# Attention on TensorE in pairs of steps, in a fused linear-attention and mixture-of-experts kernel

## The chip, the cores and the metric

The kernel runs on one core of one Trainium2 chip. The metric is device time in microseconds: three runs of the kernel before gave 607.51, 609.04 and 610.86 us, a median of 609.04. One further execution was profiled.

## What is computed

Linear attention over 8 batches of 8 heads (576 rows of 64 values each), and then a mixture of experts with one expert per row on its output. The change touches the attention alone:

```python
def phi(x):
    proj = np.einsum('bhsd,df->bhsf', x, w_phi)                 # 64 -> 128 features
    proj = proj - np.max(np.abs(proj), axis=-1, keepdims=True)
    return np.concatenate([np.exp(proj), np.exp(-proj)], axis=-1)
q_p, k_p = (phi(q), phi(k))
kv = np.einsum('bhsf,bhsd->bhfd', k_p, v)                       # sums over the rows
z = np.sum(k_p, axis=2)
num = np.einsum('bhsf,bhfd->bhsd', q_p, kv)
den = np.einsum('bhsf,bhf->bhs', q_p, z)[..., None] + 1e-06
return (num / den).astype(np.float32)
```

The rows of this go to the expert stage: a skip score and a gate choose the rows and their expert, and two matrix products with a ReLU between them follow. All matrix products of the attention are in float32.

## The kernel before

**Units, items and steps.** A unit is four heads of one batch, of k or of q; there are 16 of each. Every unit has five items: item 0 is the tail of 64 rows, items 1 to 4 are the rest. The loop at L760 goes through steps t. In each step an item of the k stream and, six steps later in its own unit, an item of the q stream pass through six stages, each with a lag (`lag` in `CFG`). The letters of `order` ('EPAZUT') give the order inside a step:

- T (L748, `st_t`): VectorE transposes the loaded rows into `xT` (L322, L324), and the next unit's load is issued on SyncE's queue.
- P, one step later (`st_proj`, L327): TensorE projects the k item and the q item into one tile `ps_P` of two banks (L347; 32 matrix instructions in the trace, 24 where one of the two is a tail). VectorE takes the largest absolute value (`m`, L354) and subtracts it (`u`, L357). There are two such tiles.
- E, three steps after T: for k, ScalarE takes the exponentials (`ek`, L372 and L373) and GpSimd sums them into `z` (L380 to L386). For q, TensorE first transposes `u` into the one bank `ps_U` (L393), and ScalarE takes the exponentials from there (`eq`, L399 and L400).
- U, four steps after T: for k, the kv sums (L415, L422) into the one bank `ps_K`; ScalarE copies them out as `kvs` at the unit's end (L426). For q, the numerators and denominators (L513, and L492 for the tails of two batches together) into a bank `ps_O`; VectorE divides in four instructions (`den`, `rec`, `xm`, `lgm`, L464 to L476). There are two banks `ps_O`.
- Z, at item 4 of k, five steps after T (L433): sums of `z` over the partitions, into a bank `ps_O`, copied by ScalarE as `zs` (L436).
- A, at item 4 of k, six steps after T (`st_aug`, L438): for each of two halves, products of `kvs` with the gate's columns and a transpose of `zs` into a bank `ps_O` (L446, L450), which two instructions of ScalarE copy into `kva` (L451, L454). The numerators of the unit's q items need both halves.

Z falls on steps 9, 14, 19, and so on, A on steps 10, 15, 20, and so on. After the last item of a batch comes work on the gate (`post`, L541): small instructions of VectorE at once, and `rank` and `index` four and seven steps later, from the list `later`.

**What sets the order.** From step 8 to step 78 TensorE's instructions stand in the order in which the loop writes them (`manual_schedule` for that engine alone). The other engines' instructions are put in order by a scheduler that estimates times and takes what it holds to be ready first. Every engine then works through its own list in that order.

**Shapes on the array.** The trace names with each matrix instruction the part of the array it uses: the projections 64\*64, the kv sums and numerators 128\*64, the sums of Z 128\*32, and the transposes, A and the gate's products 128\*128.

Of the kernel before, what the change touches and what calls it, by code (L numbers as in the profile page):

```python
# [18 lines left out]
P = 128  # L19
SLOT = 256  # L20
CFG = {'late': 1, 'gp': (0, 1, 2, 4, 6, 8, 9, 11, 12, 14, 17, 19, 21), 'rows': 9.0, 'tab': (2, 4, 5, 6, 6, 7, 8, 9, 10, 11, 12, 13, 16, 20, 32), 'ql': -2, 'q1': 0, 'vtl': 3, 'at': 6, 'cp': 0, 'seq': ('E', 'E', 'E', 'C', 'C', 'SC', 'C', 'DS', 'C', 'D'), 'lag': (1, 3, 4, 5, 6), 'post': (4, 7, 7), 'man': (8, 79), 'dnow': 0, 'off': 6, 'order': 'EPAZUT', 'direct': (), 'nb': {'K': 1, 'P': 3, 'U': 2, 'O': 2}, 'na': {'K': 1, 'P': 2, 'U': 1, 'O': 2}, 'apools': (('ld', 2), ('hl', 5), ('up', 3), ('zp', 2), ('ep', 7), ('kvp', 6), ('ac', 1), ('xp', 2)), 'mpools': (('rawp', 1), ('mx', 2), ('wseta', 1), ('mo', 2), ('wsetb', 1), ('rawq', 1))}
# [3 lines left out]
def kernel(  # L25
# [13 lines left out]
    B, H, S, D = q.shape  # L39
    NF = w_phi.shape[1]  # L40
    E = w_gate.shape[1]
# [214 lines left out]
    with actx:  # L256
# [17 lines left out]
        for b in range(B):  # L274
            for kind in ("k", "q"):
                for hq in range(NQ):
                    u = Unit()
# [19 lines left out]
        def st_loadv(u):  # L297
            u.v = ld.tile([P, 4, 4 * D], F32, tag="v", name="v", bufs=3)
            u.vt = vts[u.g % 3]
            for h in range(4):  # L300
                nc.sync.dma_start(
                    out=u.v[:, h, :].rearrange("p (g c) -> p g c", c=D),
                    in_=vu[u.g, 0:4 * P, h, :].rearrange("(g p) c -> p g c", p=P))

        def st_loadvt(u):
            for pr in range(2):
                r = slice(pr * 64, pr * 64 + 64)
                nc.sync.dma_start(
                    out=u.vt[r, pr], in_=vu[u.g, 4 * P:S].rearrange("p (n r) c -> p r n c", r=2)[:, pr])
# [409 lines left out]
        later = []  # L719
        now = [0]  # L720
# [5 lines left out]
        LP, LE, LU, LZ, LA = CFG["lag"]  # L726
# [9 lines left out]
        def run_stage(lag, f):  # L736
            for items, us, off in streams:
                s = now[0] - off - lag
                if 0 <= s < n:
                    f(*items[s])  # L740
# [7 lines left out]
        def f_t():  # L748
            for items, us, off in streams:
# [3 lines left out]
                if 0 <= s < n:  # L753
                    u, i = items[s]
                    st_t(u, i)
                    if i == 0 and s // 5 + 1 < len(us):
                        st_load(us[s // 5 + 1])

        man = None
        for t in range(n + OFF + LA):  # L760
            if CFG["man"] and t == CFG["man"][0]:
                man = ExitStack()
                man.enter_context(tc.manual_schedule(engines={mybir.EngineType.PE}))
            if CFG["man"] and t == CFG["man"][1]:
                man.close()
            now[0] = t
            for w, f in [x for x in later if x[0] <= t]:
                later.remove((w, f))
                f()
            for c in CFG["order"]:  # L770
                if c == "Z":
                    run_stage(LZ, st_z)
                elif c == "A":
                    run_stage(LA, st_aug)
                elif c == "U":
                    run_stage(LU, f_use)
                elif c == "E":
                    run_stage(LE, f_exp)
                elif c == "P":
                    st_proj()  # L780
                else:
                    f_t()
            run_stage(LU - 3, lambda u, i: st_loadv(u) if (i == 0 and u.kind == "k") else None)
            run_stage(CFG["vtl"], lambda u, i: st_loadvt(u) if (i == 0 and u.kind == "k") else None)
            if t == CFG["at"]:
                setup_aug()
            if t == 1:
                setup()
# [505 lines left out]
```

## Time and profile before

| what | value |
|---|---|
| three runs, median | 607.51, 609.04, 610.86; 609.04 us |
| the profiled execution's own time | 607.91 us |
| its span (first to last instruction) | 605.7 us |
| granted TensorE clock, mean | 0.989 |
| attention on TensorE (last numerators) | to about 341 us of the span |
| steps 10 to 75, by the groups of A | 30.22 to 288.17 us |

Times within the execution count from the span's start. A matrix instruction's duration in the trace overlaps with the next one's, so what a group of them costs is read from its start to the start of the next group. TensorE runs every float32 product as two instructions, so a count in the trace is twice that of the program's order.

### The profile page before, as it was taken

The numbers are of one execution on the slowest core, as the hardware profiler recorded it, in microseconds if no ns is written. First come the engines' busy times: TensorE is split into PE (matmuls) and PEld (weight loads), VectorE is DVE, ScalarE is ACT, GpSimd is POOL, SyncE is SP. The second block draws the span as 40 slices with busy tenths as digits, with TensorE's granted clock in tenths as the row PEclk, the third lists the DMA queues.
The fourth block names the chain that finished last, engine by engine and source line by source line (L and its number), as shares of the span: only waits on it lengthen the run. The fifth ranks groups of instructions, "written<-read, shape, count | busy, mean of one in ns | idle before, by whom it ended". The sixth has DMA issues, their size and how long they took to land. (4 is left out here: it accounts for less than half of the span.)

```text
span 605.7 us, 18767 instructions
## 1 busy us (share of the span) xinstructions
PE 567.1 (94%) x7486; PEld 466.3 (77%) x7486; DVE 502.6 (83%) x1085; ACT 330.7 (55%) x649; POOL 375.9 (62%) x399
## 2 busy tenths in 40 slices
PE   4799999999999899998989799899999998999993
PEld 2477777777777677776766699798998987988892
DVE  5799998999999989999998749956788887867841
ACT  3366565555555565564643645344557765656720
POOL 5665585495666775847865644995576674738021
PEclk9999999999999999999999999899999999999997
DMA  9998898896677567621235297489677788868500
GB/s 159 156 164 149 182 194 179 163 211 121 149 160 155 138 135 170 158 74 46 73 120 185 69 302 277 167 278 321 201 260 240 242 288 297 269 198 261 194 19 30
DMA packets 250233, 108.33 MB, mean 179 GB/s; under 512 B 192417, under 2 KB 235553, under 8 KB 250144
## 3 DMA queue, kind: packets, MB, share of 16 engines
q1 hardware_dynamic: 245632, 97.58, 62.1%
q0 software_dynamic: 3200, 9.45, 4.3%
q8 instruction: 60, 0.98, 0.7%
q10 hardware_dynamic: 1312, 0.08, 0.1%
q14 instruction: 29, 0.24, 0.1%
HBM read 83.86 MB, written 24.02 MB: 178 GB/s over the span
## 5 line engine op out<-in xcount | busy, mean ns | idle before, releaser
L380 POOL TENSOR_TENSOR z<-ek 128x512 f32<-128x512 f32 x64 | 81.2, 1272 | 77.0 <-ACT ek L373 54.3
L200 POOL TENSOR_TENSOR w<-wraw_c,w 128x256 fp32r<-128x256 f32 x108 | 97.5, 935 | 47.5 <-ACT w L195 43.9
L195 ACT ACTIVATE w<-wraw_c 128x1024 fp32r<-128x1024 f32 x96 | 97.9, 1051 | 6.9 <-DMA wraw_c<-in_moe_w_dram 6.5
L200 DVE TENSOR_TENSOR w<-wraw_c,w 128x1024 fp32r<-128x1024 f32 x69 | 90.2, 1321 | 9.5 <-ACT w L195 7.6
L354 DVE TENSOR_REDUCE m<-ps_P 128x8 f32<-128x1024 f32 (+2 forms) x86 | 88.5, 1030 | 7.1 <-PE ps_P L347 7.1
L357 DVE TENSOR_TENSOR u<-ps_P,m 128x1024 f32<-128x1024 f32 (+2 forms) x86 | 88.8, 1032 | 2.9
L347 PE MATMUL ps_P<-wsrc,xT 64*64 64x128 f32 x2048 | 79.4, 282 | 11.4 <-DMA raw<-in_k_dram 7.2
L513 PEld LDWEIGHTS ps_O<-kva,eq 128*64 128x64 f32 x2048 | 74.0, 136 | 16.4 <-issue 5.8
L513 PE MATMUL ps_O<-kva,eq 128*64 128x74 f32 x2048 | 77.4, 228 | 3.9 <-DVE lgm L476 3.8
L347 PEld LDWEIGHTS ps_P<-wsrc,xT 64*64 64x64 f32 x2048 | 57.4, 135 | 28.1 <-issue 19.2
L399 ACT ACTIVATE eq<-ps_U 128x512 f32<-128x512 f32 x64 | 37.9, 592 | 64.8 <-PE ps_U L393 64.3
L415 PE MATMUL ps_K<-ek,v 128*64 128x256 f32 x512 | 71.2, 396 | 0.0
L879 POOL DMA_INDIRECT out_dram<-o,si x22 | 34.3, 1558 | 56.6 <-DVE si L878 50.1
L946 PE MATMUL ps_O<-w,hh 128*128 128x512 f32 x160 | 64.0, 400 | 0.0
L633 POOL TENSOR_SCALAR OP<-iota_p,rkp,wcol 128x128 bf16<-128x128 f32 x62 | 48.4, 790 | 24.0 <-DVE RKH L636 17.9
L372 ACT ACTIVATE ek<-u 128x512 f32<-128x512 f32 x64 | 40.4, 631 | 39.0 <-DVE u L357 23.0
L393 PE MATMUL ps_U<-ident,u 128*128 128x128 f32 x288 | 48.9, 287 | 2.7 <-DVE u L357 2.4
L324 DVE STREAM_TRANSPOSE xT<-raw 128x512 f32<-128x512 f32 x64 | 44.7, 702 | 6.1 <-DMA raw<-in_k_dram 3.3
L415 PEld LDWEIGHTS ps_K<-ek,v 128*64 128x64 f32 x512 | 32.0, 137 | 21.1 <-issue 10.8
L950 PE MATMUL ps_O<-w,hh 128*128 128x512 f32 x120 | 47.2, 394 | 0.1
L951 PE MATMUL ps_O<-w,hlo 128*128 128x512 f32 x120 | 47.0, 392 | 0.0
L384 POOL TENSOR_TENSOR z<-z 128x512 f32<-128x512 f32 x32 | 40.7, 1273 | 2.5
(254 smaller groups left out, 1202.0 us busy)
## 6 DMA issues: line engine op xcount, KB each, us to landing
wraw_c<-in_moe_w_dram SPq DMA_DIRECT2D x96, 512.0 KB, 5.4
raw<-in_k_dram SPq DMA_DIRECT2D x64, 144.0 KB, 3.1
raw<-in_q_dram SPq DMA_DIRECT2D x64, 144.0 KB, 4.5
v<-in_v_dram SPq DMA_DIRECT2D x64, 128.0 KB, 2.8
out_dram<-xm SPq DMA_DIRECT2D x16, 512.0 KB, 6.2
xrows<-xm SPq DMA_DIRECT2D x8, 516.0 KB, 3.8
xrows<-xm SPq DMA_DIRECT2D x8, 512.0 KB, 4.2
vt<-in_v_dram SPq DMA_DIRECT2D x32, 32.0 KB, 2.5
```

The costliest lines, as they stand in the source:

```text
L195: nc.scalar.activation(out=hi, in_=raw, func=AF.Copy)
L200: eng.tensor_tensor(out=lo[:, r], in0=raw[:, r], in1=hi[:, r].bitcast(F32), op=ALU.subtract)
L347: nc.tensor.matmul(p[s * 64:s * 64 + 64, hd, (nj + j) * NF:(nj + j + 1) * NF], xT[r, g * P + s * 64:g * P + s * 64 + 64], wsrc[r], start=T ...
L354: nc.vector.tensor_reduce(out=m.rearrange("p (j h) -> p j h", h=2), in_=pv, axis=AX.X, op=ALU.max, apply_absolute_value=True)
L357: nc.vector.tensor_tensor(out=uu[:, 0:2 * nj, :].rearrange("p (j h) f -> p j h f", h=2), in0=pv, in1=m.rearrange("p (j h o) -> p j h o", h ...
L380: zeng.tensor_tensor(out=z, in0=e[:, 0:2, :], in1=e[:, 2:4, :], op=ALU.add)
L393: nc.tensor.transpose(t[:, tt * P:(tt + 1) * P], uu[:, tt, :], ident)
L415: nc.tensor.matmul(o[hd * 64:hd * 64 + 64, :], u.v[:, 2 * hd + pr, g * D:(g + 1) * D], u.e[i][:, 2 * j + hd, :], start=(g == 0), stop=False,)
L513: nc.tensor.matmul(ov[s * 64:s * 64 + 64, 2 * j + hd, :], e[:, half, j, hd, s * 64:s * 64 + 64], kva[:, half, 2 * pr + hd, :], start=(half ...
L633: (nc.vector if last else nc.gpsimd).tensor_scalar(out=OP[:, t0 + t, c, :], in0=iota_p, scalar1=rkp[:, t:t + 1], scalar2=wcol[:, NT:NT + 1 ...
L946: nc.tensor.matmul(y[sub], hh[:, t], wh[:, fi, :], start=first, stop=False)
L950: nc.tensor.matmul(y[sub], hh[:, t], wl[:, fi, :], start=False, stop=False)
```

## The change

Steps 8 to 77 are written in pairs (t even, then t+1) instead of one by one. The list `PAIR` gives the order within a pair: a letter is a stage, and 0 or 1 is the step. L stands for the due functions of the list `later`, D for the loads of v; both were outside the list before.

```diff
+        PAIR = [('L', 0), ('T', 0), ('T', 1), ('E', 0), ('P', 0), ('P', 1), ('L', 1), ('E', 1), ('A', 0), ('Z', 0), ('Z', 1), ('U', 0), ('A', 1), ('U', 1), ('D', 0), ('D', 1)]
...
-            now[0] = t
-            for w, f in [x for x in later if x[0] <= t]:
-                later.remove((w, f))
-                f()
-            for c in CFG["order"]:
-                if c == "Z":
+            first = 8 <= t < 78 and (t - 8) % 2 == 0
+            if 8 <= t < 78 and not first:
+                continue
+            for c, dt in PAIR if first else [(c, 0) for c in "L" + CFG["order"] + "D"]:
+                now[0] = t + dt
+                if c == "L":
+                    for w, f in [x for x in later if x[0] <= now[0]]:
+                        later.remove((w, f))
+                        f()
+                elif c == "Z":
...
+                elif c == "D":
+                    run_stage(LU - 3, lambda u, i: st_loadv(u) if (i == 0 and u.kind == "k") else None)
+                    run_stage(CFG["vtl"], lambda u, i: st_loadvt(u) if (i == 0 and u.kind == "k") else None)
                 else:
                     f_t()
-            run_stage(LU - 3, lambda u, i: st_loadv(u) if (i == 0 and u.kind == "k") else None)
-            run_stage(CFG["vtl"], lambda u, i: st_loadvt(u) if (i == 0 and u.kind == "k") else None)
```

No instruction is added or taken away. The arithmetic and the buffers are the same; the names' numbers and the line numbers (six more from L759 on) differ.

**Place 1: ScalarE at the A of step 20, the first step of a pair.** Before: `u_1051` is the `u` of step 19, `kva_1143` what A makes in step 20 from its two halves `ps_O_1144` and `ps_O_1150`.

```order
L399 ACTIVATE eq_1119<-ps_U_1114 128x512
L400 ACTIVATE eq_1119<-ps_U_1114 128x512
L372 ACTIVATE ek_1195<-u_1051 128x4x128
L373 ACTIVATE ek_1195<-u_1051 128x4x128
L451 ACTIVATE kva_1143<-ps_O_1144 128x4x73
L454 ACTIVATE kva_1143<-ps_O_1144 128x4
L451 ACTIVATE kva_1143<-ps_O_1150 128x4x73
L454 ACTIVATE kva_1143<-ps_O_1150 128x4
```

With the change, `u_1157` is the `u` of step 20 itself, from the first projection of this very pair; the halves of A are `ps_O_1191` and `ps_O_1197`:

```order
L399 ACTIVATE eq_1187<-ps_U_1182 128x512
L400 ACTIVATE eq_1187<-ps_U_1182 128x512
L451 ACTIVATE kva_1190<-ps_O_1191 128x4x73
L454 ACTIVATE kva_1190<-ps_O_1191 128x4
L372 ACTIVATE ek_1275<-u_1157 128x4x128
L373 ACTIVATE ek_1275<-u_1157 128x4x128
L451 ACTIVATE kva_1190<-ps_O_1197 128x4x73
L454 ACTIVATE kva_1190<-ps_O_1197 128x4
```

The copies of A's second half now stand behind exponentials of the same pair's first projection; before, both halves stood behind exponentials of the step before. All seven A on even steps read like this.

VectorE's list from the end of the pair of steps 18 and 19 to that `u`, with the change (`ps_O_1037` and `ps_O_1060` are the numerators of those two steps, `ps_P_1138` the first projection of the pair of steps 20 and 21; the four instructions of the first division stand ahead of these):

```order
L464 TENSOR_SCALAR den_1077<-ps_O_1060 128x4
L468 RECIPROCAL rec_1078<-den_1077 128x4
L475 TENSOR_TENSOR xm_553<-ps_O_1060,rec_1078 128x2x2x64
L476 TENSOR_TENSOR lgm_554<-ps_O_1060,rec_1078 128x2x18
L568 TENSOR_REDUCE L_1083<-lgm_554 128x36
L324 STREAM_TRANSPOSE xT_1427<-raw_824 128x512
L571 TENSOR_REDUCE mx_1084<-L_1083 128x4
L572 TENSOR_TENSOR d_1085<-L_1083,mx_1084 128x32
L354 TENSOR_REDUCE m_1155<-ps_P_1138 128x8
L574 SCALAR_TENSOR_TENSOR key_1089<-d_1085,desc_115 128x32
L586 TENSOR_REDUCE ss_1087<-ex_1086 128x4
L324 STREAM_TRANSPOSE xT_1589<-raw_1109 128x512
L357 TENSOR_TENSOR u_1157<-ps_P_1138,m_1155 128x1024
```

Both divisions of a pair, and gate work, now stand between the second projection of one pair and the first of the next; before, one division stood between two projections.

**Place 2: TensorE and ScalarE at the A of step 25, the second step of a pair.** TensorE with the change, from the first transposes of the pair of steps 24 and 25:

```order
L393 MATMUL ps_U<-ident,u 128x128 x2
L347 MATMUL ps_P<-wsrc,xT 64x128 x32
L393 MATMUL ps_U<-ident,u 128x128 x4
L433 MATMUL ps_O<-z,ones_f 32x256 x4
L513 MATMUL ps_O<-kva,eq 64x74 x16
L446 MATMUL ps_O<-aug,kvs 128x146 x2
L450 MATMUL ps_O<-ident,zs 128x128
L446 MATMUL ps_O<-aug,kvs 128x146 x2
L450 MATMUL ps_O<-ident,zs 128x128
L415 MATMUL ps_K<-ek,v 64x256 x4
L492 MATMUL ps_O<-kva,eqt 64x74 x16
```

Before, for the same step 25 alone, from the numerators of step 24 on:

```order
L513 MATMUL ps_O<-kva,eq 64x74 x16
L393 MATMUL ps_U<-ident,u 128x128 x4
L347 MATMUL ps_P<-wsrc,xT 64x128 x16
L446 MATMUL ps_O<-aug,kvs 128x146 x2
L450 MATMUL ps_O<-ident,zs 128x128
L446 MATMUL ps_O<-aug,kvs 128x146 x2
L450 MATMUL ps_O<-ident,zs 128x128
L415 MATMUL ps_K<-ek,v 64x256 x4
L492 MATMUL ps_O<-kva,eqt 64x74 x16
```

A now follows the numerators of step 24 directly, where transposes and a projection stood between them before. ScalarE there with the change (`u_1466` is the `u` of step 24, `ps_O_1504` the sums of Z, `ps_O_1535` and `ps_O_1541` the halves of A):

```order
L399 ACTIVATE eq_1501<-ps_U_1496 128x512
L400 ACTIVATE eq_1501<-ps_U_1496 128x512
L436 ACTIVATE zs_1509<-ps_O_1504 128x256
L372 ACTIVATE ek_1600<-u_1466 128x4x128
L373 ACTIVATE ek_1600<-u_1466 128x4x128
L451 ACTIVATE kva_1534<-ps_O_1535 128x4x73
L454 ACTIVATE kva_1534<-ps_O_1535 128x4
L451 ACTIVATE kva_1534<-ps_O_1541 128x4x73
L454 ACTIVATE kva_1534<-ps_O_1541 128x4
```

Here both halves' copies stand behind exponentials of the same pair's first projection. The second half `ps_O_1541` is given the bank of the first, `ps_O_1535`, so its products wait for the first half's copies.

## Prediction, made before the changed kernel was run

> **What bounds the kernel now.** First the page and the stretches of the span.
>
> ```profile
> span 605.7 us, 18767 instructions
> PE 567.1 (94%) x7486; PEld 466.3 (77%) x7486; DVE 502.6 (83%) x1085; ACT 330.7 (55%) x649; POOL 375.9 (62%) x399
> ...
> 150.00:200.00 50.00, 49.27 (x961) 38.49 (x957) 47.52 (x122) 28.46 (x67) 30.36 (x28) 1.00 0.74 162
> ```
>
> In the attention (columns: PE, PEld, DVE, ACT, POOL, granted clock, DMA share, GB/s) TensorE is busy 49.27 us of 50 and VectorE 47.52; the clock is whole. So two engines, not one, are nearly full. The waits from 30 to 310 us say who waits for whom (total, times, longest):
>
> ```profile
> DVE m L354 <- PE ps_P L347: 5.3, 14, 0.5
> ...
> PE ps_O L513 <- DVE lgm L476: 3.8, 3, 1.3
> PE ps_O L609 <- DVE lgm L476: 2.2, 3, 0.7
> ...
> PEld ps_P L347 <- issue: 11.9, 70, 0.3
> PEld ps_K L415 <- issue: 9.1, 52, 0.2
> ```
>
> TensorE waits for VectorE 6.0 us in 280, and VectorE for TensorE about as long: neither has slack to give. The weight loads stand idle 0.17 us (11.9 over 70, 9.1 over 52) with no releaser each time the group's shape on the array changes. The groups themselves, in the order of time:
>
> ```profile
> 162.51 0.44 PE L393 MATMUL ps_U<-ident,u 128*128 128x128 f32 x2
> 162.88 1.10 PE L347 MATMUL ps_P<-wsrc,xT 64*64 64x128 f32 x32
> 163.91 0.64 PE L433 MATMUL ps_O<-z,ones_f 128*32 128x256 f32 x8
> 164.48 1.25 PE L513 MATMUL ps_O<-kva,eq 128*64 128x74 f32 x32
> 165.66 0.66 PE L393 MATMUL ps_U<-ident,u 128*128 128x128 f32 x4
> 166.24 1.10 PE L347 MATMUL ps_P<-wsrc,xT 64*64 64x128 f32 x32
> 167.28 0.77 PE L446 MATMUL ps_O<-aug,kvs 128*128 128x146 f32 x4
> ...
> 168.07 0.74 PE L446 MATMUL ps_O<-aug,kvs 128*128 128x146 f32 x4
> ...
> 168.85 1.08 PE L415 MATMUL ps_K<-ek,v 128*64 128x256 f32 x8
> ...
> 171.67 0.67 PE L347 MATMUL ps_P<-wsrc,xT 64*64 64x128 f32 x16
> 172.15 0.40 PE L347 MATMUL ps_P<-wsrc,xTt 64*64 64x128 f32 x8
> 172.48 1.08 PE L415 MATMUL ps_K<-ek,v 128*64 128x256 f32 x8
> 173.40 0.60 PE L422 MATMUL ps_K<-ekt,vt 128*64 128x256 f32 x4
> 173.83 1.20 PE L513 MATMUL ps_O<-kva,eq 128*64 128x74 f32 x32
> 174.96 0.66 PE L393 MATMUL ps_U<-ident,u 128*128 128x128 f32 x4
> ```
>
> From start to start: projections 1.03 us for 32 and 0.81 for 24, transposes 0.58 for 4 and 0.37 for 2, kv sums 0.92 and 0.43, numerators 1.13, A 1.57 (0.79 for its first half), Z 0.57. Twenty steps last 79.92 us: the A at 167.28 is the eighth, and the twelfth is this one.
>
> ```profile
> 247.20 0.77 PE L446 MATMUL ps_O<-aug,kvs 128*128 128x146 f32 x4
> ```
>
> **Term 1, what the pairs save: changes of shape.** The projections cost 0.22 us more for 8 more instructions, so 0.0275 each and 0.88 for 32; the other 0.15 is a fixed part. Transposes: 0.21 for 2 more, so 0.42 for 4, and 0.16 fixed. The kv sums, with the same shape behind them, take 0.92 for 8 and 0.43 for 4: no fixed part. I take 0.15 us per change; the bounds are 0.10 (a fixed part partly of the group's own) and 0.19. A single step has three changes (transposes, projections, kv sums and numerators, transposes); a pair had six and now has four. A on an even step falls between groups of its own shape and saves one, A on an odd step stands between two of the other and costs one. So 35 pairs times 2 is 70 changes, 10.5 us (7.0 to 13.3).
>
> [...]
>
> **Term 2, waits of TensorE that go.** The 6.0 us above stand where numerators follow a Z, or a gate product comes, in the step after other numerators, and VectorE has not emptied the bank. In a pair two projections lie between; I count them as gone (bounds 0 and 6.0).
>
> **Term 3, new waits at the A.** The rows for it, VectorE and ScalarE:
>
> ```profile
> 151.56 0.18 DVE L572 TENSOR_TENSOR d<-L,mx 128x32 f32<-128x32 f32 x1
> 151.78 0.19 DVE L574 SCALAR_TENSOR_TENSOR key<-d,desc 128x32 f32<-128x32 f32 x1
> ...
> 163.30 0.15 DVE L464 TENSOR_SCALAR den<-ps_O 128x4 f32<-128x4 f32 x1
> ...
> 164.04 0.18 DVE L476 TENSOR_TENSOR lgm<-ps_O,rec 128x36 f32<-128x36 f32 x1
> 164.14 1.22 DVE L354 TENSOR_REDUCE m<-ps_P 128x8 f32<-128x1024 f32 x1
> 165.27 0.70 DVE L324 STREAM_TRANSPOSE xT<-raw 128x512 f32<-128x512 f32 x1
> 165.90 1.19 DVE L357 TENSOR_TENSOR u<-ps_P,m 128x1024 f32<-128x1024 f32 x1
> 167.01 0.14 DVE L464 TENSOR_SCALAR den<-ps_O 128x4 f32<-128x4 f32 x1
> ```
>
> ```profile
> 188.37 0.64 DVE L568 TENSOR_REDUCE L<-lgm 128x36 f32<-128x288 f32 x1
> ```
>
> ```profile
> 167.38 0.63 ACT L372 ACTIVATE ek<-u 128x512 f32<-128x512 f32 x1
> 167.90 0.63 ACT L373 ACTIVATE ek<-u 128x512 f32<-128x512 f32 x1
> 168.42 0.41 ACT L451 ACTIVATE kva<-ps_O 128x292 f32<-128x292 f32 x1
> 168.71 0.19 ACT L454 ACTIVATE kva<-ps_O 128x4 f32<-128x4 f32 x1
> 168.95 0.41 ACT L451 ACTIVATE kva<-ps_O 128x292 f32<-128x292 f32 x1
> ```
>
> Start to start: a division 0.84, `m` 1.13, a transpose 0.63, `u` 1.11, the gate's first sum 0.6, its small ones 0.1 to 0.22; two `ek` 1.04, one half's copies 0.5. At 168.42 the copy starts at the end of the `ek`, though A's first half had ended: ScalarE keeps its order.
>
> [...]
>
> *A on an even step* (place 1), clock from the pair's first transposes. TensorE: transposes 0.59, projections 0.93 and 0.77, transposes 0.5, A 1.57, one kv sum 0.92: at 5.3 us it has the tails' numerators (L492, in every second batch), or after the second kv sum (1.34) at 6.6 the other numerators, and both need A's second half. VectorE has to begin with the two divisions of the pair before, since the second `u` there ends about now: that pair's first projections are ready at 1.6 us of its 7.0 (0.59 + 0.93, and 0.1), and `m`, `u`, `m`, a transpose and `u` take 1.13 + 1.11 + 1.13 + 0.63 + 1.11 = 5.1, to 6.7 or a little later. So: two divisions 1.68, then 0.6, a transpose 0.63, 0.37, `m` 1.13, 0.3, a transpose 0.63, `u` 1.11, together 6.45. Then `ek` 1.04 and copies 0.5, with 0.1 for the hand-over: 8.1. TensorE waits 2.8 us in three pairs, 1.5 in four: 14.4 us. If the first division is done before the pair begins, 0.84 less each (8.5); if VectorE is 0.5 later, 17.9.
>
> *A on an odd step* (place 2). TensorE: transposes 0.37, projections 0.93 and 1.0, transposes 0.59, Z 0.57, numerators 1.13, half of A 0.79: at 5.4 it wants the second half. The first projection is ready at 1.4; `m` 1.13, two transposes 1.26, `u` 1.11, `ek` 1.04, copies 0.5, hand-overs 0.2: 6.6. A wait of 1.2, plus how late VectorE begins; the pair before ends with a division behind its gate work, so 0.4. Seven times 1.6 is 11.2 us (8.4 without lateness, 14.7 with 0.9).
>
> Term 3 is 25.6 us (16.9 to 32.6). While TensorE waits here, VectorE runs dry some microseconds later, so the other one does not make it good. The page's loads (last column: us to landing):
>
> ```profile
> raw<-in_k_dram SPq DMA_DIRECT2D x64, 144.0 KB, 3.1
> raw<-in_q_dram SPq DMA_DIRECT2D x64, 144.0 KB, 4.5
> ```
>
> What else moves costs nothing: VectorE's transposes and SyncE's loads go ahead of the projections by up to a step, and no transfer is among VectorE's waits from 30 to 310 us; without that cover a late load would cost up to its landing time, 3.1 us for k and 4.5 for q. The ranks of the gate stand before transposes of their own shape.
>
> **The sum.** 25.6 - 10.5 - 6.0 = +9 us, on the profiled execution's own 607.9, which makes 617. The median of the three runs is 1.1 above that execution: 618. The expert stage starts where the attention ends, and moves along.
>
> **Rivals.**
> - *A larger hold.* VectorE falls further behind and the same place-1 order also holds the sums of Z on odd steps: `zs` stands behind `ek` of the same pair too, with some 0.6 us to spare by the rows above. If VectorE is 0.9 later at all fourteen A: 25.6 + 12.6 - 7.0 = +31; half-way, about 628. For: VectorE is 95% busy. Against: each wait of TensorE lets it catch up.
> - *Faster.* VectorE reaches `u` in time (two divisions fit while TensorE is still at the last numerators, and the transposes ahead of `u` prove done earlier), so that the holds fall under 0.4 us. Then 10.5 + 6.0 is saved, but VectorE's own work bounds it: it waited for TensorE 5.3 us for `m` and little else, so the gain ends at 6 to 8. Price: 602. It decides if ScalarE is past `ek` at 5.3 us of the pair; the rows put it at 7.6.
> - *No change.* Holds of 16.9 against savings of 16.5: 609. It needs the lower bound of term 3 throughout.
>
> That the pairs don't come about is no rival: TensorE's list shows them.
>
> **Chances.** Forecast 0.60, larger hold 0.16, faster 0.13, no change 0.11. A measurement of this kernel tells about 0.5% (3 us) from nothing, so slower 0.76, same 0.11, faster 0.13. The likeliest one's own range is 611 to 626; with both sides up to 2 in 10 left out, 605 to 631.
>
> **What would show it.** Term 1: fewer changes, projections 32 + 32 in about 1.9 us. Term 2: no wait of L513 behind a Z. Term 3: waits of TensorE at L492 and L513 for `kva` (L454), and at A (L446) for the same, 1 to 3 us each, seven of either kind, with `ek` running just before the copies; VectorE waiting longer for `ps_P`. The prediction is wrong if the copies of A end before TensorE is there.

## The result

The changed kernel takes 633.76 us (median of 4 runs, 631.12 to 638.98) against 608.27 us (median of 4 runs of the kernel before in the same comparison, 607.24 to 610.86): a ratio of 1.042, 95% interval 1.035 to 1.050. The forecast was 618, with 605 to 631 as its range: the direction is right, the size is not, and the median lies above the range.

The page of the profiled execution (633.93 us):

```profile
span 631.9 us, 18716 instructions
PE 572.5 (91%) x7486; PEld 476.1 (75%) x7486; DVE 505.5 (80%) x1085; ACT 331.5 (52%) x649; POOL 373.4 (59%) x399
...
PEclk9899999989799989899989979999999999999998
```

The span is 26.2 us longer, with the same instructions on TensorE. TensorE is busy 5.4 us longer (572.5, before 567.1), VectorE 2.9. The row of the granted clock, forty slices of 15.8 us, has a seven (158 to 174 us) and five eights among the 22 slices of the attention; the kernel before has nines alone there.

The waits of TensorE from 30 to 330 us (total, times, longest):

```profile
PE ps_O L446 <- ACT kva L454: 10.3, 7, 1.9
PE ps_O L492 <- ACT kva L454: 10.0, 6, 2.6
PE ps_O L513 <- ACT kva L454: 5.7, 3, 1.9
PE ps_O L513 <- DVE rm L627: 1.4, 3, 0.5
PE ps_O L513 <- DVE cs L699: 1.1, 1, 1.1
```

The three waits for `kva` that the prediction named are there, at the three lines that it named, and together last 26.0 us. The waits for `lgm` at L513 and L609 are gone. VectorE now waits for TensorE's numerators:

```profile
DVE den L464 <- PE ps_O L513: 12.2, 10, 3.0
DVE den L464 <- PE ps_O L492: 6.0, 5, 1.5
DVE xT L324 <- PE ps_P L347: 5.8, 10, 1.8
```

One hold at an A on an odd step, on TensorE and then on ScalarE (start, duration, the idle time before it in brackets):

```profile
226.60 0.77 PE L446 MATMUL ps_O<-aug,kvs 128*128 128x146 f32 x4 [1.87 <-ACT kva L454]
227.20 0.27 PE L450 MATMUL ps_O<-ident,zs 128*128 128x128 f32 x1
227.40 1.69 PE L415 MATMUL ps_K<-ek,v 128*64 128x256 f32 x8
229.02 0.45 PE L653 MATMUL ps_O<-rm,OP 128*128 128x32 bf16 x10
229.31 1.09 PE L393 MATMUL ps_U<-ident,u 128*128 128x128 f32 x4
```

```profile
225.03 0.63 ACT L372 ACTIVATE ek<-u 128x512 f32<-128x512 f32 x1 [1.39 <-DVE u L357]
225.56 0.61 ACT L373 ACTIVATE ek<-u 128x512 f32<-128x512 f32 x1
226.08 0.39 ACT L451 ACTIVATE kva<-ps_O 128x292 f32<-128x292 f32 x1
226.38 0.17 ACT L454 ACTIVATE kva<-ps_O 128x4 f32<-128x4 f32 x1
```

ScalarE waits 1.39 us for `u`, takes both exponentials and only then copies A's first half, whose matrix work was done at 224.73; TensorE stands for 1.87 us. This is the mechanism of the prediction. What it did not have comes behind: the eight kv sums at 227.40 take 1.62 us from start to start, where 0.92 is usual, and the four transposes at 229.31 take 1.02 for 0.58. The clock in that stretch and in another one (columns: PE, PEld, DVE, ACT, POOL, granted clock, DMA share, GB/s):

```profile
227.70:231.10 3.40, 3.40 (x38) 2.13 (x38) 0.59 (x3) 0.89 (x4) 3.40 (x3) 0.51 1.14 200
162.90:169.70 6.80, 5.17 (x54) 5.12 (x56) 3.67 (x13) 2.24 (x6) 3.80 (x3) 0.50 0.79 178
```

TensorE runs at half its clock there. One such stretch of 3.4 us lies at 26.4 us, in the first pairs. Between 70 and 320 us there are six more, at 77.6, 139.0, 162.9, 227.7, 251.6 and 316.5 us, 3.4 or 6.8 us long, 27.2 us in all; each begins at most 1.2 us after a hold of 1.8 us or more ended, or within one. The kernel before has none in its attention.

Where the time went is seen best over forty steps without the ends, from the A of step 25 to that of step 65. The same stretch of the kernel before, and of the changed one:

```profile
87.40:247.20 159.80, 155.79 (x2973) 120.78 (x2971) 150.49 (x361) 93.22 (x219) 108.91 (x101) 1.00 0.74 158
```

```profile
93.70:271.10 177.40, 159.88 (x2973) 127.80 (x2971) 153.44 (x361) 93.52 (x218) 108.90 (x101) 0.94 0.63 136
```

These forty steps last 17.6 us longer: TensorE's idle time grows from 4.0 to 17.5 us (159.80 - 155.79, 177.40 - 159.88), and its busy time by 4.1 in spite of forty changes of shape fewer.

### The profile page after: what moved, and what is told of

It reads as the page before. It is cut to its first block, busy times and chain, and to the rows that moved or that the text cites. A ratio compares the mean times of both kernels' runs of the same rounds, so it can differ in the third digit from the quotient of the medians.

```text
span 631.9 us, 18716 instructions
## 1 busy us (share of the span) xinstructions
PE 572.5 (91%) x7486; PEld 476.1 (75%) x7486; DVE 505.5 (80%) x1085; ACT 331.5 (52%) x649; POOL 373.4 (59%) x399
## 5 line engine op out<-in xcount | busy, mean ns | idle before, releaser
L200 POOL TENSOR_TENSOR w<-wraw_c,w 128x256 fp32r<-128x256 f32 x108 | 98.9, 949 | 48.2 <-ACT w L195 46.8
L200 DVE TENSOR_TENSOR w<-wraw_c,w 128x1024 fp32r<-128x1024 f32 x69 | 91.8, 1345 | 9.7 <-ACT w L195 8.4
L513 PEld LDWEIGHTS ps_O<-kva,eq 128*64 128x64 f32 x2048 | 76.5, 139 | 20.6 <-ACT kva L454 6.2
L513 PE MATMUL ps_O<-kva,eq 128*64 128x74 f32 x2048 | 80.3, 231 | 8.4 <-ACT kva L454 5.7
L347 PE MATMUL ps_P<-wsrc,xT 64*64 64x128 f32 x2048 | 74.6, 282 | 12.8 <-DVE xT L324 7.1
L347 PEld LDWEIGHTS ps_P<-wsrc,xT 64*64 64x64 f32 x2048 | 59.1, 137 | 23.9 <-issue 16.0
L415 PE MATMUL ps_K<-ek,v 128*64 128x256 f32 x512 | 75.8, 417 | 0.0
L885 POOL DMA_INDIRECT out_dram<-o,si x22 | 31.1, 1415 | 58.2 <-DVE si L884 51.7
L415 PEld LDWEIGHTS ps_K<-ek,v 128*64 128x64 f32 x512 | 35.9, 145 | 20.5 <-issue 10.4
L393 PE MATMUL ps_U<-ident,u 128*128 128x128 f32 x288 | 50.4, 294 | 0.1
L384 POOL TENSOR_TENSOR z<-z 128x512 f32<-128x512 f32 x32 | 40.7, 1273 | 2.3
```

Of the source, the lines that this page charges most:

```text
L200: eng.tensor_tensor(out=lo[:, r], in0=raw[:, r], in1=hi[:, r].bitcast(F32), op=ALU.subtract)
L347: nc.tensor.matmul(p[s * 64:s * 64 + 64, hd, (nj + j) * NF:(nj + j + 1) * NF], xT[r, g * P + s * 64:g * P + s * 64 + 64], wsrc[r], start=T ...
L393: nc.tensor.transpose(t[:, tt * P:(tt + 1) * P], uu[:, tt, :], ident)
L415: nc.tensor.matmul(o[hd * 64:hd * 64 + 64, :], u.v[:, 2 * hd + pr, g * D:(g + 1) * D], u.e[i][:, 2 * j + hd, :], start=(g == 0), stop=False,)
L513: nc.tensor.matmul(ov[s * 64:s * 64 + 64, 2 * j + hd, :], e[:, half, j, hd, s * 64:s * 64 + 64], kva[:, half, 2 * pr + hd, :], start=(half ...
```

## Experiments

All whole times are medians; "beside" gives the kernel before on the same chip. The forty steps are always those from the A of step 25 to that of step 65; they, and all intervals between two A, are read from the one profiled execution of each kernel.

### 1. A's copies ahead of the exponentials

Theory after the result: the holds come from ScalarE's order alone, and the half clock comes from the holds. The edit puts the exponentials `ek` behind the last copy of A that is written before them, on ScalarE; TensorE's and VectorE's lists in the attention stay as they are in the changed kernel.

```diff
-            nc.scalar.activation(out=e[:, :, 0, :], in_=uu[:, 0:nt, :], func=AF.Exp)
-            nc.scalar.activation(out=e[:, :, 1, :], in_=uu[:, 0:nt, :], func=AF.Exp, scale=-1.0)
+            with tc.issue_after(kva_last[0].ins) if kva_last[0] else ExitStack():
+                nc.scalar.activation(out=e[:, :, 0, :], in_=uu[:, 0:nt, :], func=AF.Exp)
+                nc.scalar.activation(out=e[:, :, 1, :], in_=uu[:, 0:nt, :], func=AF.Exp, scale=-1.0)
```

> The changed kernel with one difference: on ScalarE the copies of A (L451, L454) go ahead of the exponentials of k that stood before them in place 1 and place 2; TensorE's and VectorE's lists in the attention stay as they are. Theory (the holds at A make the loss, directly and by the half clock that follows them): the 26.0 us of TensorE's waits for kva fall to about 5 us (the second half of A still waits for its bank, some 0.7 us in seven pairs), the half-clock stretches before 345 us go, and the time falls from 634 to 600 us (594 to 608), under that of the kernel before. Rival (grouping in pairs itself slows TensorE or VectorE): it stays above 615. Rival (VectorE is the bound either way): 605 to 612, with VectorE busy at least 48 of 50 us.

The same edit in the kernel before, which has no such holds:

> The kernel before with the same edit on ScalarE (the copies of A ahead of the exponentials of the step). Theory: nothing there waits for these copies, so 608 us, within 3. Rival (the order on ScalarE costs something in single steps too): faster by over 3 us.

Measured: 621.49 us in pairs (ratio 1.021, 1.020 to 1.023), 610.23 in the kernel before (1.003, 1.002 to 1.004); beside 608.45. So the holds and what follows them are worth 12.3 us, and the edit alone brings nothing. The forty steps:

```profile
89.90:255.20 165.30, 153.11 (x2975) 121.04 (x2971) 153.75 (x361) 93.57 (x218) 109.33 (x101) 1.00 0.69 148
```

The clock is whole in these steps. TensorE's busy time is 6.8 us less than in the changed kernel (153.11 for 159.88): that is the half clock. Its idle time is 5.3 less. But 12.2 us of idle time remain, and the kernel stays 13 us above the one before, where the theory had it below. The waits of TensorE from 30 to 330 us:

```profile
PE ps_O L446 <- ACT kva L454: 4.0, 7, 0.6
PE ps_O L513 <- DVE rm L627: 3.2, 6, 0.6
PE ps_O L653 <- DVE lgm L476: 2.8, 3, 1.0
PE ps_O L492 <- DVE lgm L476: 2.7, 3, 0.9
PE ps_P L347 <- DVE u L357: 2.5, 3, 0.9
PE ps_O L513 <- DVE cs L699: 2.4, 1, 2.4
PE ps_O L492 <- ACT kva L454: 2.3, 3, 0.8
```

For `kva` 6.3 us are left of 26.0; in their place TensorE waits 13.6 us for VectorE. The theory was right on the holds and wrong on what lies beneath them; of the rivals, it is the one of a pairing that is slow in itself (over 615) whose range holds the time. Outside the forty steps the clock is not whole: it is half from 23.2 to 30.0 us, in the first pairs, and from 310.0 us on, behind the longest wait of the list (start, duration, idle time before it; then the stretch):

```profile
309.73 2.06 PE L513 MATMUL ps_O<-kva,eq 128*64 128x74 f32 x32 [2.37 <-DVE cs L699]
```

```profile
310.00:313.40 3.40, 3.40 (x48) 2.92 (x46) 1.65 (x11) 0.47 (x1) 1.91 (x2) 0.50 0.11 15
```

### 2. TensorE kept at work in the holds

In the changed kernel, fourteen transposes of the identity, into a bank that is overwritten afterwards, ahead of the first numerators behind an A on an even step. They take no wait away; they only fill it.

```diff
+            if 8 <= now[0] < 78 and (i == 0 and now[0] % 10 == 0 or i == 1 and now[0] % 10 == 1 and u.b % 2 == 0):
+                for _ in range(14):
+                    nc.tensor.transpose(o[:, 0:P], ident, ident)
```

> The changed kernel with 14 transposes of the identity (1.5 us at whole clock, results overwritten) put before the first numerators after A in the seven pairs with A on an even step, where TensorE otherwise stands still 1.9 to 2.6 us waiting for kva. The holds stay; only the idle time in them is filled. Theory that the idle time lowers the clock: the half-clock stretches at 77.6, 162.9 and 251.6 us go (13 to 17 us of them), and the time falls by 4 to 8 us from 634. Rival (the clock falls for another reason, or costs nothing): 634 within 2, and the half-clock stretches stay. Waits for kva at L492 and L513 that the trace shows fall by about 1.5 us each in either case.

Measured: 630.43 us (1.036; beside 608.45), 3.3 less than the changed kernel, a little under the lower end expected. The half clock at 77.6, 162.9 and 251.6, which lay at the longest holds, is gone, and the three intervals from the A of step 20, 40 and 60 to the next fall from 23.2, 24.0 and 24.1 us to 21.5. The one from step 40, in the changed kernel and with the holds filled:

```profile
158.30:182.40 24.10, 20.76 (x360) 17.38 (x358) 19.45 (x52) 10.68 (x26) 11.25 (x12) 0.86 0.57 126
```

```profile
159.10:180.60 21.50, 19.83 (x373) 16.37 (x371) 19.30 (x52) 10.66 (x26) 11.20 (x12) 1.00 0.61 136
```

The whole times alone are too close to show this (the intervals are 1.034 to 1.038 and, for the changed kernel, 1.035 to 1.050); the stretches of the trace do. So work without any use makes the filled stretches faster; the full clock behind the holds is what changed there. One half-clock stretch, at 227.7 us in the changed kernel, went too, though the hold of 1.87 us ahead of it was not filled and is still there; so a hold of this length does not always bring half clock. From the A of step 15 to that of step 75 the gain is 8.1 us (262.9 to 254.8); it was partly given back at both ends (1.7 us in steps 10 to 15, 1.7 in steps 75 to 80).

### 3. The changes of shape put back

The run of experiment 1 with a product of another shape (128 by 8, on the whole array) between the two projections of each pair, 70 changes more:

```diff
+            if 8 <= now[0] < 78 and now[0] % 2: nc.tensor.matmul(p[:, 0, 0:E], ones_b, Stot, start=True, stop=True)
```

> The first of these kernels with a small bf16 product (128x8, whole array, its result is overwritten) between the two projections of each of the 35 pairs, so that each pair has two more changes of shape on the array. By term 1 of the prediction (0.15 us a change) and about 0.03 us for the product itself it is 11.5 us slower than the kernel without it (8 to 14). Rival (VectorE or ScalarE sets the pace once the holds are gone): under 4 us slower.

Measured: 624.19 us (1.026, 1.025 to 1.027; beside 608.45), 2.7 more than without: 0.04 us per change in time. By term 1 it would have been 10 or more; 2.7 lies in the range of the rival (under 4). In the forty steps TensorE's busy time grows by 4.2 us (153.1 to 157.3) for forty changes and twenty products, and its idle time falls by 2.7. Either a change costs far less than 0.15, or TensorE is not what sets the pace; experiments 5 and 6 decide that.

### 4. Which part of the pairing is paid for

Three versions of experiment 1. In the first, only steps 20 to 69 are written in pairs:

```diff
-            first = 8 <= t < 78 and (t - 8) % 2 == 0
+            first = 20 <= t < 70 and t % 2 == 0
...
```

> The first run with A's copies ahead of the exponentials (621.5 us), with only steps 20 to 69 written in pairs, the rest one by one as in the kernel before. In that run 3.4 us of the loss lay ahead of the A of step 10 and 3.6 us between the A of step 75 and that of step 80; 5.2 us lay in the 65 steps between, 0.08 per step. Theory (the ends lose because the pairs reach into steps in which transposes, loads and the last expert preparations differ): without them about 608.5 + 50 x 0.08 = 612.5 us (610 to 615). Rival (each change from single steps to pairs and back costs this, wherever it stands): 618 to 622, with the loss moved to about steps 20 and 70.

In the second only the two projections stay together, in the third only the two steps' sums and numerators:

```diff
+        PAIR = [('L', 0), ('T', 0), ('T', 1), ('E', 0), ('P', 0), ('P', 1), ('A', 0), ('Z', 0), ('U', 0), ('L', 1), ('E', 1), ('A', 1), ('Z', 1), ('U', 1), ('D', 0), ('D', 1)]
...
+        PAIR = [('L', 0), ('T', 0), ('E', 0), ('P', 0), ('L', 1), ('T', 1), ('E', 1), ('P', 1), ('A', 0), ('Z', 0), ('Z', 1), ('U', 0), ('A', 1), ('U', 1), ('D', 0), ('D', 1)]
```

> The same run with A's copies first, but only the two projections of a pair stay together: kv sums and numerators of the first step come before the transposes of the second, so five changes of shape per pair, not four. Theory (the two steps' numerators together are what is still paid for: TensorE waits for VectorE's lgm at L492 and L653, because both divisions come in one bunch): 612 to 616 us, and no wait of TensorE for lgm at L492. Rival (the two projections together are what is paid for, since the second cannot begin before VectorE's u of the tile before it is out): 620 to 624. By term 1 of the prediction alone (0.15 us per change, 35 more): 626.7.

> The same run with A's copies first, but only the two steps' kv sums and numerators stay together; transposes and projection of each step come one by one, five changes of shape per pair. Theory (numerators together are what is paid for): 620 to 624 us. Rival (projections together are what is paid for): 612 to 616, and the wait of L347 for u gone.

Measured, beside 608.70: 616.26 us (1.013, 1.010 to 1.016), 623.63 (1.025, 1.023 to 1.028) and 633.45 (1.040, 1.037 to 1.043).

The first lies between theory and rival. The ends are gone, as the theory had it: the A of step 10 comes at 29.83 us (33.58 in experiment 1, 30.22 in the kernel before), and steps 75 to 80 last 21.51 us (25.01 and 21.42). So 5.2 us were lost by the first and the last pairs. The half clock that experiment 1 has at both ends (6.8 and 3.4 us) is not in this trace before 350 us, nor is the wait for `cs`. The early one is not the pairs' alone: another kernel of experiment 5 with single steps up to step 19 has half clock from 22.2 to 29.0 us too, and comes to the A of step 10 at 31.72 us. But the pairs in between cost more than the 4 us I had counted: from the A of step 20 to that of step 70 it is 207.4 us, in the kernel before 199.7.

The other two show no half that is to blame. The second has the time of its rival (620 to 624); the third lies above both ranges. Both are slower than experiment 1, where projections and sums are both together. TensorE's waits from 30 to 310 us say where they lose, with the projections alone together,

```profile
PE ps_O L446 <- ACT kva L454: 7.0, 7, 1.0
PE ps_O L513 <- ACT zs L436: 6.2, 6, 1.0
PE ps_U L393 <- ACT eq L400: 5.2, 3, 1.7
```

and with the sums alone together:

```profile
PE ps_U L393 <- ACT eq L400: 8.9, 22, 1.2
PE ps_O L612 <- DVE OH L581: 3.4, 3, 1.1
```

With the projections alone together, TensorE waits for ScalarE's copies of A and of Z and, three times, for the one bank `ps_U`; no wait for `lgm` at L492 is left, as the theory had it, but 18.4 us of others are there. With the sums alone together, the second step's transposes come right behind the first's projection and wait for `ps_U` in 22 steps; this kernel also falls to half clock within the forty steps (a mean of 0.97), which the other two do not. My question (which half) was the wrong one: each order makes its own waits.

### 5. Is VectorE the pace? GpSimd and VectorE in each other's way

VectorE's busy time in the forty steps is 153.8 us in experiment 1 and 150.5 in the kernel before, for the same instructions. The trace shows two that became long (others became shorter, L581 from 0.66 to 0.44 us and L587 from 0.38 to 0.15). From the groups of experiment 1 and of the kernel before, both from 30 to 310 us (count, total, mean in ns):

```profile
L620 DVE TENSOR_TENSOR Stot<-Stot,st 128x8 bf16<-128x8 bf16 x6 | 6.5, 1082 | 0.0
L572 DVE TENSOR_TENSOR d<-L,mx 128x32 f32<-128x32 f32 (+1 forms) x6 | 5.8, 974 | 0.2
```

```profile
L572 DVE TENSOR_TENSOR d<-L,mx 128x32 f32<-128x32 f32 (+1 forms) x6 | 1.1, 186 | 0.0
L620 DVE TENSOR_TENSOR Stot<-Stot,st 128x8 bf16<-128x8 bf16 x6 | 0.9, 147 | 0.0
```

One of them on VectorE in experiment 1, and GpSimd at the same time:

```profile
206.95 1.15 DVE L620 TENSOR_TENSOR Stot<-Stot,st 128x8 bf16<-128x8 bf16 x1
208.03 0.18 DVE L627 TENSOR_TENSOR rm<-ps_O,OH 128x40 f32<-128x40 f32 x1
```

```profile
206.81 1.27 POOL L380 TENSOR_TENSOR z<-ek 128x512 f32<-128x512 f32 x1 [1.88 <-issue]
```

An instruction on eight values per partition ends at 208.10, when GpSimd's sum ends at 208.08. So I cut GpSimd's sums into quarters, in three kernels, with every other engine's list unchanged:

```diff
-            zeng.tensor_tensor(out=z, in0=e[:, 0:2, :], in1=e[:, 2:4, :], op=ALU.add)
+            [zeng.tensor_tensor(out=z[:, j, h], in0=e[:, j, h], in1=e[:, 2 + j, h], op=ALU.add) for j, h in cut]
```

(`cut` are the four pieces of 128 columns; L384 and L386 likewise.)

> The run with A's copies first (621.5 us), with each of GpSimd's sums for z (L380, L384, L386; 128x512, 1.27 us each) cut into four instructions of 128x128. Every other engine's list is the same. Why: in that run VectorE's small instructions with both inputs in SBUF take long when they start while L380 runs, and end with it (L572 0.97 us a piece where the kernel before has 0.19, L620 1.08 where it has 0.15; L581, which stretches in the kernel before, less: 0.44 for 0.66). Theory (this collision is part of what is still paid, since VectorE is near its limit): L572 and L620 fall to about 0.45 us, some 1.1 us per batch less, and the whole to 615 to 618. Rival (the stretched instructions lie beside waits of VectorE that are there anyway): 620.5 to 622.

> The same cut of GpSimd's sums in the kernel before, whose VectorE loses some 0.95 us at L581 in every second batch and 0.4 at L587. Theory: not over 2 us faster, 606.5 to 608.5. Rival (the cut helps both alike, so the change has no part in it): as much faster as the run with the change, 3 us or more.

> Pairs in steps 20 to 69 alone with A's copies first (616.3 us) and GpSimd's sums in quarters. Theory (collision on the path, five batches in pairs): 611 to 613. Rival (not on the path): 615.5 to 617.

Measured, beside 608.36: 622.9 us (1.025, 1.022 to 1.027), 607.6 in the kernel before (0.9995, 0.998 to 1.001), and 614.51 with pairs in steps 20 to 69 (1.010, 1.008 to 1.012). The expected 3 to 6 us did not come: the full pairs took 1.4 us more than without the cut (622.9 for 621.49, above even the rival's range), the pairs in steps 20 to 69 took 1.8 less (614.51 for 616.26, between theory and rival), and their single runs overlap with those of the uncut kernels. The kernel before lies in the theory's range. The edit did only half of what I wanted. The groups of the first of the three, from 30 to 310 us:

```profile
L572 DVE TENSOR_TENSOR d<-L,mx 128x32 f32<-128x32 f32 (+1 forms) x6 | 8.4, 1405 | 0.2
L620 DVE TENSOR_TENSOR Stot<-Stot,st 128x8 bf16<-128x8 bf16 x6 | 1.5, 243 | 0.0
```

`Stot` fell to 0.24 us, but `d` rose to 1.4. One of these, and GpSimd's pieces:

```profile
194.11 1.51 DVE L572 TENSOR_TENSOR d<-L,mx 128x40 f32<-128x40 f32 x1
```

```profile
193.87 1.70 POOL L380 TENSOR_TENSOR z<-ek 128x128 f32<-128x128 f32 x4
```

VectorE's instruction waited out all four pieces, which follow each other without a gap and take longer together (1.70 us for 1.27). The forty steps fell by 1.4 us (165.3 to 163.9), and from the A of step 75 to that of step 80 2.9 were lost (25.01 to 27.87). Such a loss is in all three kernels, and lies behind one instruction, L714, on sixteen values and once in the attention. In the kernel before, and with pairs in steps 20 to 69 and the cut:

```profile
292.12 0.38 DVE L714 TENSOR_TENSOR acc<-acc 128x16 f32<-128x16 f32 x1
```

```profile
297.51 7.35 DVE L714 TENSOR_TENSOR acc<-acc 128x16 f32<-128x16 f32 x1
```

Eighteen of GpSimd's pieces, back to back, began while it waited. With the cut it takes 5.81, 5.35 and 7.35 us in the three kernels, and steps 75 to 80 last 27.87, 24.58 and 26.83 us for 25.01, 21.42 and 21.51. So the whole times hide what the cut gains elsewhere: from the A of step 20 to that of step 70 it is 2.1 us in the full pairs (207.5 to 205.3), 2.2 in the kernel before (199.7 to 197.5) and 3.5 with pairs in steps 20 to 69 (207.4 to 203.9). With the cut on both sides the pairs of steps 20 to 69 are still 6.4 us behind the single steps there, for 7.7 without. So the collision is real, and the kernel before pays for it too; its full share of the loss is not settled by these runs, since the cut takes it away for one instruction and makes it worse for others.

The more direct test is to lighten VectorE: `m` over 64 of 128 features, in pairs and one by one. The scheduler's estimates change with it, so that some of VectorE's and ScalarE's other instructions come in another order too, in this experiment and the next; what that does by itself was not tried.

```diff
-                out=m.rearrange("p (j h) -> p j h", h=2), in_=pv, axis=AX.X, op=ALU.max, apply_absolute_value=True)
+                out=m.rearrange("p (j h) -> p j h", h=2), in_=pv[:, :, :, 0:NF // 2], axis=AX.X, op=ALU.max, apply_absolute_value=True)
```

> The run with A's copies first (621.5 us), with VectorE's largest value (m, L354, 1.10 us a piece, one per step) taken over 64 of the 128 features, so that VectorE has some 0.5 us less to do in every step; this leaves out a part of the computation, and the routing of rows may differ. Theory (VectorE sets the pace once the holds are gone, so that the saved changes of shape cannot show): from the A of step 25 to that of step 65 165.3 us become 156 to 159, near TensorE's busy 153.1, and the whole 608 to 612. Rival (TensorE's own waits for ScalarE and for the order of the pair set it): the 40 steps stay over 162 us.

> The kernel before with VectorE's largest value (m, L354) taken over 64 of the 128 features, as in the run of the pairs, where the 40 steps from the A of step 25 to that of step 65 then took 155.2 us; it leaves out that part of the computation, and the rows go to other experts, so only the attention is compared. Theory (with slack on VectorE the pairs pay: fewer changes of shape): the same 40 steps take 157 to 159 us here (159.85 in the kernel before, 155.8 of them TensorE's busy time). Rival (the changes of shape are worth nothing even then): 154.5 to 156.

The whole times, 834.15 and 832.43 us (the second a single run), say nothing, since the rows go to other experts. The forty steps, in pairs:

```profile
89.10:244.30 155.20, 151.15 (x2975) 120.44 (x2971) 137.39 (x360) 92.95 (x218) 108.02 (x99) 1.00 0.74 161
```

and one by one:

```profile
87.90:244.20 156.30, 155.12 (x2975) 121.02 (x2971) 132.85 (x361) 93.84 (x219) 109.22 (x101) 1.00 0.75 161
```

With 0.41 us less on VectorE per step (153.75 - 137.39 over 40) the pairs come down by 10.1 us from 165.3, and the waits for `lgm` go with them (2.7 us at L492 become 0.2). That is a little below the theory's range (156 to 159) and far from the rival's 162: in experiment 1 VectorE's work limits the pace. The single steps fall by 3.5 us, to 156.3, below what I expected (157 to 159) and near the rival's range (154.5 to 156): TensorE now has 1.2 us of idle time in 156.3, so it is the bound there. And here, with slack on VectorE, the pairs are ahead for the first time, by 1.1 us in forty steps: they save 4.0 us of TensorE's busy time (155.12 - 151.15; 0.10 for each of 40 changes of shape) and give 2.9 back as waits (4.05 idle for 1.18).

### 6. Less VectorE work, whole runs

The same idea in whole kernels: the addition of 1e-6 to the denominators is left out, and `rec` reads the bank itself.

```diff
-            nc.vector.tensor_scalar(
-                out=den.rearrange("p (t o) -> p t o", o=1), in0=o[:, :, NA1:NAUG],
-                scalar1=1e-6, scalar2=None, op0=ALU.add,
+            nc.vector.reciprocal(
+                out=rec.rearrange("p (t o) -> p t o", o=1),
+                in_=o[:, :, NA1:NAUG],
             )
-            nc.vector.reciprocal(out=rec, in_=den)
```

> Pairs in steps 20 to 69 with A's copies first (616.3 us), and the addition of 1e-6 to the denominators (den, L464, 0.15 us a piece, 64 of them) left out, so that rec reads the denominators straight from the bank: some 0.2 us less for VectorE per step. The list of VectorE's and ScalarE's instructions is also put in a somewhat different order by the scheduler. Theory (VectorE sets the pace there): over half of 50 x 0.2 comes out, 607 to 612 us, and the gap to the kernel before with the same edit shrinks below 5. Rival: 614 to 617.

> The kernel before with the same addition left out. Theory (TensorE, busy 155.8 of 159.8 us in 40 steps, sets the pace here): 605 to 608.5 us. Rival (VectorE limits it as much as it limits the pairs): 600 to 604, and the gap between the two stays at 8.

Measured, beside 608.83: 607.86 us with pairs in steps 20 to 69 (0.999, 0.998 to 1.000) and 603.26 in the kernel before (0.991, 0.988 to 0.993). The pairs fall by 8.4 us from 616.3, into the theory's range (607 to 612), and so equal the kernel before; the gap to the single steps with the same edit is 4.6 us, under 5 as the theory said. But the kernel before gained 5.6 us, more than the theory's range (605 to 608.5) allows and inside the rival's (600 to 604): VectorE limits it too, only less. Its forty steps:

```profile
87.40:242.40 155.00, 154.64 (x2974) 120.68 (x2970) 143.37 (x325) 92.78 (x219) 109.08 (x100) 1.00 0.76 165
```

TensorE is idle 0.4 us of 155. This version, single steps without `den`, takes less time than both kernels of this case, by under 1% of the one before; it leaves out the 1e-6 of the reference.

The forty steps of the main kernels side by side, in us:

| kernel | time | TensorE busy | TensorE idle | VectorE busy |
|---|---|---|---|---|
| before | 159.8 | 155.8 | 4.0 | 150.5 |
| the change | 177.4 | 159.9 | 17.5 | 153.4 |
| copies first | 165.3 | 153.1 | 12.2 | 153.8 |
| copies first, changes put back | 166.8 | 157.3 | 9.5 | 154.2 |
| half of `m`, pairs | 155.2 | 151.2 | 4.1 | 137.4 |
| half of `m`, single steps | 156.3 | 155.1 | 1.2 | 132.9 |
| no `den`, pairs | 159.3 | 152.2 | 7.1 | 145.9 |
| no `den`, single steps | 155.0 | 154.6 | 0.4 | 143.4 |

## Why the prediction was right in direction and wrong in size

**What bounds the kernel.** "Neither has slack to give" was right, and truer than I used it. Experiment 6 bears it out in the kernel before: 0.18 us less on VectorE per step (150.49 - 143.37 over 40) made it 5.6 us faster, though TensorE seemed busy 49 us of 50.

**The step that failed: the sum.** It took terms 1 and 2, 16.5 us, off the time, as if TensorE alone set it, and it had no term for the granted clock or for the first and last pairs. By that sum a kernel with the fewer changes and without the holds is 16.5 us faster than the kernel before. Experiment 1, which has the fewer changes and 6.3 of the 26.0 us of holds left, is 13.0 us slower. So the forecast "slower" came true for half of its reason only. That term 3 alone, 25.6 us, is so near the measured 25.5 is a coincidence: taking 19.7 us of the holds away, and the half clock behind them, gave 12.3 us.

**Term 3, the holds: right in place and cause, and near in total.** 26.0 us where 25.6 were forecast. Place 1: 15.7 (10.0 at L492 and 5.7 at L513) for 14.4. There six pairs hold where seven were forecast, and each for longer: 3.35 us (0.76 and 2.59) for 2.8, and 1.9 for 1.5. Place 2: 10.3 for 11.2, in seven waits. The cause is shown: with A's copies ahead of the exponentials 6.3 us of the 26.0 are left. What is wrong is the price: the prediction counted each hold as time in full, but the 19.7 us taken away were not 19.7 us of time, since TensorE then waits for VectorE instead.

**Term 2, the waits that go: right in the changed kernel, but not for good.** The waits for `lgm` are gone and 2.5 us of others at L513 stand in their place, for 6.0. Without the holds (experiment 1) TensorE waits 13.6 us for VectorE, at `lgm` too; so it is the holds, in which VectorE can catch up, that kept these waits away.

**Term 1, the changes of shape: mis-sized, and taken for time.** Forecast 0.15 us each and 10.5 in all. Measured in TensorE's busy time, forty fewer save 2.7 us (before against experiment 1) to 4.0 (with VectorE lightened), 0.07 to 0.10 each, so 5 to 7 for 70. The idle 0.17 us of the weight loads, on which I leaned, is not what a change costs, and it does not stand at each of them: from 30 to 310 us the kernel before has it at the projections (L347, 11.9 us over 70) and the kv sums (L415, 9.1 over 52), but none with `issue` at the transposes (L393), whose shape differs from that of the numerators before them; the changed kernel has it there 21 times (3.8 us from 30 to 330 us). The runs show that a change costs something here, 0.07 to 0.10 us of busy time; what TensorE does at one they do not show. The larger error is that the sum took this saving off the time although VectorE was nearly as full as TensorE: with VectorE as it is, experiment 1 has the saving in busy time and still lasts 5.5 us longer in forty steps. The prediction's rival "faster" bounded its gain by VectorE's own work; the forecast did not.

**What the sum left out.** First, the clock. The prediction noted that it was whole and took that over. Half clock cost 6.8 us of TensorE's busy time in forty steps, and experiment 2 shows for the three longest holds that it comes from TensorE standing still. Second, the ends: the first and last pairs cost 5.2 us (experiment 4); I had looked at steps 10 to 75 alone. In the trace of experiment 1 they have 10.2 us at half clock and the wait of 2.4 us for `cs`; how much of the early half clock is due to the pairs stays open.

**The account.** Of the 25.5 us, 12.3 go with the holds and the half clock (experiment 1), 5.2 with the first and last pairs (experiment 4), and 7.6 remain with pairs in steps 20 to 69; the last 0.4 is the difference of the kernel before between these measurements (608.27 and 608.70). That VectorE's pace is a limit there is borne out by leaving out `den`: the gap of 7.6 becomes 4.6, with a somewhat different order on VectorE and ScalarE besides. Why it is slower in pairs than in single steps is shown in part only: in forty steps it works 3.3 us longer on the same instructions, two of which run into GpSimd's sums for longer, and is idle 2.2 us longer (11.5 for 9.3). How much of the 7.6 is due to the collision stays open.

**The rest.** "The expert stage moves along" holds: from the second half of the last A to the end of the span it is 272.8 us before and 272.3 after. Of the rivals, the larger hold gave 628, the nearest number, but the holds were not larger. The other two had too small holds.

## What to carry to other kernels

Where two engines are nearly full, as here, a saving on one of them need not be time (experiment 1 saves 2.7 us of TensorE's busy time in forty steps and lasts 5.5 us longer); test it by lightening the other before counting it. When work of one engine is grouped, follow the other engines' order instruction by instruction, since a group's first result queues up behind work that the next group needs. Count a hold of TensorE of about 2 us at more than its length if the granted clock may fall behind it (between 70 and 320 us of the changed kernel, six of nine holds of 1.8 us or more had half clock for 3.4 or 6.8 us at them), and read the clock again in every new trace.

## What the hardware did that I had not expected

**The clock falls after short idle times.** Of the changed kernel's holds between 70 and 320 us, the three at L492 (0.76 us, then 2.59 with little work between) and three of 1.8 to 1.87 us at L446 are followed by half clock for 3.4 or 6.8 us. Three of 1.9 us at L513 and three of 1.2 us at L446 are not. The starts of the six stretches are 61.4, 23.9, 64.9, 23.9 and 64.9 us apart, which is near 18, 7, 19, 7 and 19 times 3.41 us (239.0 us over 70), about the length of the shortest stretch; why, these runs do not show. The longest idle time was 2.59 us, less than any of the stretches that came with it. TensorE's busy time just ahead does not tell the holds with half clock from those without. Counted in steps of 3.41 us from these starts, the one ahead of the stretch at 162.9 us, and one that holds a wait at L513 with no half clock behind it, are these:

```profile
159.50:162.90 3.40, 1.68 (x16) 0.81 (x14) 3.40 (x8) 1.57 (x5) 0.26 (x1) 1.00 1.13 258
207.30:210.70 3.40, 1.50 (x28) 1.13 (x26) 3.40 (x10) 1.75 (x6) 0.03 (x1) 1.00 1.07 246
```

TensorE was busy 1.68 us in the first and 1.50 in the second. The 3.4 us ahead of the six stretches have 0.90 to 1.72 us of busy time, those that hold the three waits at L513 have 1.50 each; so what decides between them stays open.

**Some of VectorE's small instructions wait out GpSimd's sum, and a run of short ones keeps them waiting.** VectorE's `Stot`, 0.15 us in the kernel before, took 1.15 us in experiment 1 and ended at 208.10 us, when GpSimd's sum ended at 208.08. With GpSimd's sums in four pieces back to back, VectorE's `d` (0.19 us in the kernel before) ended at 195.62 us and the last piece at 195.57: it waited for the end of all four (1.51 us) and not for that of one (0.43, a quarter of 1.70). `acc` at L714 waited while eighteen pieces began and ended 7.35 us after its start, with more pieces still to follow; what let it in there these runs do not show.
